# Three orders in a fused RWKV and feed-forward kernel: shifts behind scales, weight loads earlier, one late step rearranged

## The chip, the cores and the metric

The kernel runs on one core of a Trainium2 chip. The metric is the device time of one execution in microseconds (us). The engines are TensorE (PE in the profile, PEld for its weight loads), VectorE (DVE), ScalarE (ACT), GpSimd (POOL) and SyncE (SP), which here only issues DMAs.

## What is computed

The first half is RWKV-6 attention over 4 batches, 8 heads, 768 tokens and a head dimension of 48; the second half a feed-forward block with 384 model and 2048 hidden columns, whose activation is h times erf of softplus of h.

```python
for t in range(S):
    kt, vt, rt, wt = (k[:, :, t], v[:, :, t], r[:, :, t], w[:, :, t])
    cur = np.einsum('bhd,bhe->bhde', u[None] * kt, vt)
    y[:, :, t] = np.einsum('bhd,bhde->bhe', rt, state + cur)
    state = wt[:, :, :, None] * state + np.einsum('bhd,bhe->bhde', kt, vt)
...
h = x @ w_in
sp = np.maximum(h, 0.0) + np.log1p(np.exp(-np.abs(h)))
g = h * erf(sp)
return (g @ w_out).astype(np.float32)
```

The weights `w_in` and `w_out` come as 64-bit floats, and the kernel makes them 32-bit floats on the chip.

## The kernel before, in words

**Steps.** The tokens are worked off in 12 steps, s = 0 to 11. A step holds 128 tokens of two batches (16 heads), and one tile `in` with r and k, one `w` and one `v`. The first step has a function of its own, `attend_first` (L833); steps 1 to 4 go through `attend` (L962), steps 5 to 11 through `attend_late` (L782). The second step of the change is s = 1, the sixth s = 5. Beside the attention of step s, TensorE works on the feed-forward block of earlier steps in pieces: a piece of `hidden` (L1087) of step s - 1 is 12 matmuls with `w_in_sb` (line L1120 in the profile) and one ScalarE copy out of PSUM (L1129); its PSUM tiles are two that take turns. A piece of `project_fast` (L1227) of step s - 3 is 8 matmuls with `w_out_sb` or `mixed` (L1242).

**Levels of a step.** In `attend` the tokens within a block of 64 are handled in levels 1 to 6. A level is 64 small matmuls (`level_products`, L641) on r and k, then `scale` (L334, VectorE), which multiplies r and k in place by products of w so that the next level's matmuls can use them, then `take_level`, which copies the products where a mask holds: on VectorE up to level 5 (L651), at level 6 by two ScalarE copies (L658). After level 6, `from_own` (L673) multiplies the result with v. `prepare` of the next step is a generator whose parts are run in between: among them GpSimd's totals of w (L408) and ScalarE's products with u (L386, L389).

**Conversion of the weights.** `convert` (L223) cuts w_in and w_out into 8 chunks each, chunks 0 to 7 being w_in. A chunk goes through these stages, which the code names by letters:
- `l`, load (L231): two DMAs of 384 KB into a tile `words`, of which there are three, taking turns. A load can be made to wait by a marker, a copy of one element into the tile on GpSimd (L244) or ScalarE (L242).
- `b`, the base (L259 for w_in): ScalarE, from `words` into PSUM. From chunk 2 on all bases use the one tile `y`.
- `r`, the low words (L267): ScalarE, from `words` into `rest`, of which there are two.
- `h`, the shift (L276): VectorE, from the base into the weights.
- `o`, the add (L289): GpSimd, adds `rest`.

Piece n of the hidden work of step 0 needs chunk n whole. In the second step, chunks 2 to 7 are converted while the levels run. At each level from 2 on, a GpSimd copy of one element of k (L994) makes the adds wait until `scale` is done.

**Order of the work.** All engines' orders are written out by hand: each engine takes its instructions in the order of the program, DMAs on SP's queue too. An instruction that waits holds up what stands behind it on its engine. In the second step, `place(n)` is called after each level; it sends bases, low words and loads by the table `CONVERT` (L1477), then one hidden piece.

**The late steps.** In `attend_late`, the function `run` (L1566) works off a string of tokens at seven places ("front", "near", 0 to 4), from `USUAL` or, for a step that has an entry there, from `LATE`. `P` is a project piece, `H` a hidden piece, `F` the next part of `prepare` of the next step (in the sixth step, among others, the scales of levels 1 to 3 of the seventh), `s` a softplus on a chunk of hidden values (L1076, with a table load), `ey` and `ep` the erf of it into the tile `y` or a bank `pp` (L1080), `m` the VectorE multiply that follows (L1085). `kABx` copies a quarter of the hidden values of step s - 2 to lane x, `y` or `pp`, in PSUM (L1200), and `S1` to `S4` are VectorE sums of quarters (L1219 to L1225). Pieces 3, 4, 6 and 7 of a project end with a copy or an add out of PSUM: L1253 (piece 3) and L1256 (piece 4) on ScalarE, L1262 (piece 6) and L1267 (piece 7) on VectorE. The PSUM tiles of the project are those that the hidden pieces take next.

Of the kernel before, what the change touches and what calls it, by code (L numbers as in the profile page):

```python
# [17 lines left out]
P = 128  # L18
# [22 lines left out]
DIRECT = 4  # L41
# [21 lines left out]
def kernel(  # L63
# [23 lines left out]
    KT = DM // P  # L87
# [65 lines left out]
    def load_w(s):  # L153
        ws[s] = ins.tile([P, JP, C], FP32, name="w")
        nc.sync.dma_start(out=ws[s][:], in_=rkw[s][:, 2])
# [34 lines left out]
    def load_v(s):  # L190

        vt = loaded[s][1]
        nc.sync.dma_start(out=vt[:], in_=v[s])
# [493 lines left out]
    def through_state(s, xT):  # L687

        c, in_t, _, _, S, _, _ = parts_of(s)
        for h, state in enumerate((S, middle)):  # L690
            if not (c or h):
                continue
            t = slice(h * HC, (h + 1) * HC)
            for j, q in ((0, 2), (1, 2), (1, 0), (0, 0)) if not s else np.ndindex(NJ, NP // 2):
                q = q if not s else 2 * q
                for e in range(NE):
                    for p in (q + e, q + 1 - e):
                        n = j * NP + p
                        nc.tensor.matmul(  # L699
                            y[at(e, p), e, p // 2, j, t],  # L700
                            lhsT=state[rows(e), n, :],
                            rhs=(in_t[:, 0, n] if s else first_pair(0, n))[rows(e), t],
                            start=False, stop=True, skip_group_check=True,
                        )

        y3 = att.tile([P, UNIT], FP32, name="y3", bufs=1)
        nc.scalar.copy(y3[:].rearrange("p (j t) -> p j t", j=NJ), y[:, 1, 1])
        parts = y[:, 0, 0], y[:, 0, 1], y[:, 1, 0]
        by_kk = [xT[:, kk, :].rearrange("p (j t) -> p j t", j=NJ) for kk in range(KT)]
        if not s:  # L710

            def hop():
                for kk in range(KT):
                    nc.tensor.matmul(
                        parts[kk], lhsT=apart[:, kk],
                        rhs=y3[:].rearrange("p (j t) -> p j t", j=NJ),
                        start=False, stop=True, skip_group_check=True,
                    )
                for kk in range(KT):
                    nc.scalar.copy(by_kk[kk], parts[kk])  # L720
                stages["l"](3, xT[:, KT - 1, 0:1], True)
                stages["l"](4)
                load_w(2)

            turns["hop"] = hop
            return
        for kk in range(KT):
            nc.scalar.copy(by_kk[kk], parts[kk])
        by_scalar = {(kk, 1) for kk in range(KT) if s <= DIRECT}
        for kk in range(KT):  # L730
            n = D // KT
            for e in range(NE):
                queue = nc.scalar if (kk, e) in by_scalar else nc.sync
                queue.dma_start(
                    out=xT[e * EP + D : (e + 1) * EP, kk, :],
                    in_=y3[e * EP + kk * n : e * EP + (kk + 1) * n, :],
                )
# [95 lines left out]
    def attend_first(xT):  # L833
# [5 lines left out]
        c, _, vt, made, S, S_next, ends = parts_of(0)  # L839
# [73 lines left out]
        stages["b"](1, 1)  # L913
        fence()
        stages["l"](2, seen[:, 0:1])
        load_v(1)
        stages["h"](0)
        stages["h"](0)
        ps = [[products([P, NE, JP, HC], 1 - e)[:, e] for e in range(NE)]]
# [15 lines left out]
        def pending():  # L935
            part = products([P, NE, JP, HC], turns["next"])[:, 0]
            state_part(0, kT, ps + [[part] * NE], (1,))
            nc.vector.tensor_add(S_next[both], faded[1][both], part[both, :, :D])
            load_third()
            stages["l"](5, S_next[:, 0, 0:1])  # L940

        turns["pending"] = pending

# [18 lines left out]
    def attend(s, xT, early, place, behind):  # L962

        c, in_t, vt, made, S, S_next, ends = parts_of(s)
        K = in_t[:, 1]
        RK = by_pair(in_t)


        following = prepare(s + 1) if s + 1 < n_steps else iter(())
        own = made if s >= DIRECT else att.tile([P, NH, HC], FP32, name="own")  # L970

        if s == DIRECT:
            next(following)
        for level in range(near_log(s) + 1 if s == DIRECT else 1, LOG + 1):
            rk = by_pair(made) if level == 1 else RK
            pp = turns.pop("pp", None) or products([P, NE, JP, HC])
            if s == level == 1:
                level_products(pp, rk, level, range(NP))
                turns.pop("hop")()
                level_products(pp, rk, level, range(NP, JP))  # L980
                send("br")
            elif s != 2 or level != 2:
                level_products(pp, rk, level)
            if level == LOG and s == DIRECT:
                spread_blocks(s + 1, pp)
            if s == 1 and 2 < level:
                stages["h"](level + 1)
            scale(s, level)
            if s == 1 and level == 2:
                turns.pop("pending")()  # L990
            if s == 1 and level < 3:
                stages["h"](level + 1)
            if s == 1 and level > 1:
                nc.gpsimd.tensor_copy(out=block_sb[:, 0:1], in_=K[:, 0, 0:1])  # L994
                for i in {2: (2, 3)}.get(level, (level + 1,)):
                    stages["o"](i)
            if s != 1:
                early(level - 1)
            got = pp[:].rearrange("p e n t -> p (e n) t")
            if level == 1:  # L1000
                nc.vector.tensor_mul(
                    own[:], got, first[:, None, :].to_broadcast([P, NH, HC])
                )
            else:
                take_level(own, pp, level)
            later_on = (s, level) in ((1, 4), (DIRECT, LOG))
            if level > 1 and not later_on:
                next(following, None)
            if (s, level) == (DIRECT, LOG - 1):
                next(following, None)  # L1010
            if s == 2 and level == 1:

                def ahead():
                    turns["pp"] = products([P, NE, JP, HC])
                    level_products(turns["pp"], RK, 2)

                turns["ahead"] = ahead
            place(level - 1)
            if later_on:
                next(following, None)  # L1020
            if (s, level) == (DIRECT - 1, LOG - 1):
                nc.gpsimd.tensor_copy(out=first[:, 0:1], in_=own[:, 0, HC // 4 : HC // 4 + 1])
                mixing.send(nc.gpsimd)
            if s == 1 and level in (3, 4):
                nc.sync.dma_start(out=loaded[2][0][:, level - 3], in_=rkw[2][:, level - 3])

        from_own(s, own, 1)
        ps = products([P, JP, P])
        for n in range(JP):
            nc.tensor.transpose(ps[:, n, :], K[:, n, :], ident[:])  # L1030
        kT = att.tile([P, NH, D], FP32, name="kT", bufs=1)
        nc.scalar.copy(
            kT[:].rearrange("p (e n) d -> p e n d", e=NE),
            ps[:].rearrange("p n (e d) -> p e n d", e=NE)[..., :D],
        )
        if c:
            nc.gpsimd.tensor_mul(
                faded[0][:], S[:], ends[:, :, 0:1].to_broadcast([P, JP, D])
            )
        next(following, None)  # L1040
        place(LOG)
        if s == 2:
            mixing.send(nc.vector)
        if s == DIRECT - 1:
            advance(1)

        ps = products([P, NC, JP, HC])
        ps = [[ps[:, h]] * NE for h in range(NC)]
        state_part(s, kT, ps)
        from_own(s, own, 0)  # L1050
        if c:
            nc.vector.tensor_add(middle[both], faded[0][both], ps[0][0][both, :, :D])
        else:
            nc.vector.tensor_copy(middle[both], ps[0][0][both, :, :D])
        if s == DIRECT - 1:
            blend(s - 2, 1)
        nc.gpsimd.tensor_mul(faded[1][:], middle[:], ends[:, :, 1:2].to_broadcast([P, JP, D]))
        nc.vector.tensor_add(S_next[both], faded[1][both], ps[1][0][both, :, :D])
        for _ in following:
            pass  # L1060
        place(LOG + 1)
        through_state(s, xT)
        behind()
# [356 lines left out]
    def in_order(s, k):  # L1420
# [7 lines left out]

    STAGES_LATE = ("front", "near", 0, 1, 2, 3, 4)
    LATE = {  # L1430
        n_steps - 1: (
            "s P", "m w", "ey P m s P P ep P", "m P P", "", "", ""
        ),
# [71 lines left out]
    with tc.manual_schedule(  # L1505
# [78 lines left out]
        s = n_steps  # L1584
# [108 lines left out]
```

## Time and profile before

| what | us |
|---|---|
| median of 3 runs | 577.24 |
| lowest and highest of them | 577.05 and 582.2 |
| the profiled execution's own time | 579.45 |
| its span, from the first to the last instruction | 577.7 |
| PE busy | 568.4 |
| DVE busy | 441.9 |
| ACT busy | 357.8 |
| POOL busy | 245.9 |

Times in the profile count from the start of the span. A line of the timeline gives the start, the duration, the engine, the line of the kernel, the operation, its output and inputs with their sizes, how many instructions are merged, and in brackets how long the engine was idle before it and whose end released it. A line of the waits gives who waited, for whom, the sum in us, how often, and the longest. The granted TensorE clock was 0.999 of full speed over the span.

### The profile page before, as it was taken

The page shows a single profiled execution, that of the slowest core. Times are in us where ns is not written, and L with a number is a line of the kernel's source. Part 1 is how long each engine was busy: PE and PEld are TensorE (multiplying, and loading weights), DVE is VectorE, ACT ScalarE, POOL GpSimd, SP SyncE. Part 2 cuts the span into 40 slices and gives each one's busy share as a digit, 9 for nine tenths or more (in the row PEclk, how much of TensorE's full clock was granted, in tenths as well). Part 3 has the DMA queues.
Part 4 walks back from the last instruction along what each step waited for, and adds up shares of the span by engine and source line. Part 5 has one row for each costly group of instructions (what it writes and reads, how often), then busy time and mean ns, then how long its engine had stood idle before and what let it go on. Part 6 is the DMA issues. An engine that isn't in the chain of part 4 may idle for free.

```text
span 577.7 us, 16717 instructions
## 1 busy us (share of the span) xinstructions
PE 568.4 (98%) x7336; PEld 503.7 (87%) x7336; DVE 441.9 (76%) x475; ACT 357.8 (62%) x488; POOL 245.9 (43%) x265
## 2 busy tenths in 40 slices
PE   8999999999999999999999999999999999999997
PEld 6677787678998988998998998898898899988997
DVE  8766786999899998699699599599599527256640
ACT  3648877645458847757756766766766661388700
POOL 4557381632885884384284185175173000000000
PEclk9999999999999999999999999999999999999999
DMA  8696671440436315145245235234232201000000
GB/s 265 188 332 228 206 232 45 188 159 8 146 70 180 108 58 164 35 156 169 34 143 175 40 126 191 39 112 167 43 111 82 48 8 37 1 1 2 27 28 27
DMA packets 54081, 63.24 MB, mean 109 GB/s; under 512 B 35160, under 2 KB 40568, under 8 KB 52984
## 3 DMA queue, kind: packets, MB, share of 16 engines
q1 hardware_dynamic: 53624, 61.98, 34.4%
q8 instruction: 57, 0.93, 0.7%
q10 hardware_dynamic: 384, 0.20, 0.1%
q14 instruction: 16, 0.13, 0.1%
HBM read 52.39 MB, written 8.69 MB: 106 GB/s over the span
## 4 chain that ended last, share of the span: by engine, by line
PE 85%; DVE 3%; issue 0%; DMA 0%; POOL 0%; ACTq 0%; DVEq 0%; POOLq 0%
PE m L1120 33%; PE m L1242 32%; PE pp L1330 4%; PE m L1152 4%; PE pp L641 4%; PE y L1330 2%; PE y L673 2%; PE y L699 2%; PE pp L748 1%; DVE h L1085 1%; PE pp L1030 1%; PE pp L1242 0%; DVE sums L529 0%; DVE in L334 0%; DVE words L494 0%
## 5 line engine op out<-in xcount | busy, mean ns | idle before, releaser
L1120 PE MATMUL m<-xT,w_in_sb 128*128 128x256 f32 x960 | 215.4, 382 | 0.3 <-DMA xT<-y 0.2
L1120 PEld LDWEIGHTS m<-xT,w_in_sb 128*128 128x128 f32 x960 | 179.7, 190 | 26.4 <-ACT h L1129 1.0
L334 DVE TENSOR_TENSOR in<-in,tot_sb 128x1024 f32<-128x1024 f32 (+1 forms) x55 | 78.8, 1432 | 12.5 <-PE pp L641 11.1
L1129 ACT COPY h<-m 128x512 f32<-128x512 f32 x80 | 46.3, 578 | 48.2 <-PE m L1120 47.9
L1242 PE MATMUL m<-mixed,h 128*128 128x192 f32 x320 | 56.7, 331 | 0.0
L1242 PE MATMUL m<-w_out_sb,h 128*128 128x192 f32 x320 | 56.1, 329 | 0.0
L1242 PE MATMUL m<-w_out_sb,room 128*128 128x192 f32 x304 | 52.6, 326 | 0.7 <-ACT o L1253 0.7
L1242 PEld LDWEIGHTS m<-mixed,h 128*128 128x128 f32 x320 | 51.8, 190 | 1.0
L1242 PEld LDWEIGHTS m<-w_out_sb,h 128*128 128x128 f32 x320 | 52.0, 190 | 0.5
L1242 PEld LDWEIGHTS m<-w_out_sb,room 128*128 128x128 f32 x304 | 49.9, 190 | 1.0 <-ACT o L1253 1.0
L1080 ACT ACT_TABLE_LOAD x30 | 38.5, 1283 | 9.1 <-DVE h L1085 8.6
L641 PEld LDWEIGHTS pp<-in 48*48 48x48 f32 (+4 forms) x2368 | 30.1, 120 | 12.5 <-issue 6.1
L463 POOL TENSOR_TENSOR words<-words,own 128x384 f32<-128x384 f32 x21 | 31.0, 1475 | 22.7 <-DVE words L494 13.0
L504 POOL TENSOR_TENSOR words<-words 128x384 f32<-128x384 f32 x28 | 39.7, 1447 | 0.0
L1076 ACT ACT_TABLE_LOAD x30 | 38.5, 1283 | 1.8 <-issue 1.3
L456 POOL TENSOR_TENSOR own<-rest 128x384 f32<-128x384 f32 x7 | 9.7, 1384 | 61.5 <-ACT o L1248 61.5
L641 PE MATMUL pp<-in 48*48 48x32 f32 (+4 forms) x2368 | 33.9, 206 | 1.9 <-DVE in L334 1.9
L504 POOL TENSOR_TENSOR rk<-words 128x384 f32<-128x384 f32 x28 | 33.4, 1221 | 0.0
L529 DVE TENSOR_REDUCE sums<-rk 128x16 f32<-128x768 f32 (+2 forms) x31 | 31.6, 1021 | 0.0
L408 POOL TENSOR_TENSOR tot_sb<-tot_sb 128x256 f32<-128x256 f32 (+4 forms) x50 | 28.8, 576 | 3.8
L1076 ACT ACTIVATE room<-h 128x1024 f32<-128x1024 f32 x28 | 29.6, 1057 | 0.3
L1200 ACT COPY y<-h 128x1024 f32<-128x1024 f32 x12 | 12.2, 1018 | 26.7 <-DVE h L1085 16.9
(206 smaller groups left out, 997.2 us busy)
## 6 DMA issues: line engine op xcount, KB each, us to landing
in<-in_rkw SPq DMA_DIRECT2D x8, 1024.0 KB, 5.3
words<-in_moe_w_in SPq DMA_DIRECT2D x16, 384.0 KB, 6.8
words<-in_moe_w_out SPq DMA_DIRECT2D x16, 384.0 KB, 5.4
words<-in_rk_rows SPq DMA_DIRECT2D x8, 768.0 KB, 6.9
w<-in_rkw SPq DMA_DIRECT2D x11, 512.0 KB
v<-in_v SPq DMA_DIRECT2D x12, 384.0 KB, 5.7
out<-o SPq DMA_DIRECT2D x23, 192.0 KB, 3.2
in<-in_rkw SPq DMA_DIRECT2D x7, 512.0 KB, 5.3
```

The source lines that it names most:

```text
L334: nc.vector.tensor_mul(halves, halves, view(tots[level - 1], 0, [[1, n], [2, nb], [0, half]]))
L408: nc.gpsimd.tensor_mul(new, pair[:, :, 0], pair[:, :, 1])
L463: engine.tensor_mul(to, to, of[:, :, None, :].to_broadcast([P, NEAR // 2 // half, half, D]))
L504: engine.tensor_mul(to[:, i], r[:, half:], k[:, part * rows + i, None].to_broadcast([P, half, D]),)
L529: nc.vector.tensor_reduce(out=to, in_=of, axis=mybir.AxisListType.X, op=ALU.add)
L641: nc.tensor.matmul(to, lhsT=rk(1, n)[rows(e), s0 : s0 + m], rhs=right, start=True, stop=True,)
L1076: nc.scalar.activation(sp_room, chunks[0], AF.Softplus)
L1080: nc.scalar.activation(at, sp_room, AF.Erf)
L1120: nc.tensor.matmul(ps[:, ff, :], lhsT=w_in_sb[:, g * FG + f + ff, kk * P : (kk + 1) * P], rhs=xT[:, kk, :], start=kk == 0, stop=kk == KT - 1,)
L1129: nc.scalar.copy(h[:, f : f + FT, :], ps[:])
L1242: nc.tensor.matmul(to, lhsT=a[:, f], rhs=b[:, f], start=start and f == 0, stop=f == FG - 1, skip_group_check=True,)
L1330: nc.tensor.matmul(to[:, e], lhsT=a[:, 2 * i + e], rhs=b, start=start and not k, stop=True, skip_group_check=True,)
```

## The change

In `hop`, at level 1 of the second step, the loads of chunks 3 and 4 and of w of the third step become the load of chunk 4 alone, with the ScalarE marker that chunk 3 had. Chunk 3 is loaded in the first step, behind chunk 2, without a marker, where v of the second step stood. Chunk 5, which waited for the new state by a GpSimd marker, is loaded at the end of level 1 without a marker. w of the third step and v of the second are loaded at the end of level 3.

At levels 3 to 6 of the second step the shift goes from ahead of `scale` to behind `take_level`, and the marker copy of k and the add go behind the shift. Level 2 keeps its order.

The sixth step gets an entry in `LATE`. Against `USUAL`, a `P` goes ahead of the `s` at place 0, and two `F` go from the end of place 1 to behind `S1` at place 2.

```diff
@@ hop
-                stages["l"](3, xT[:, KT - 1, 0:1], True)
-                stages["l"](4)
-                load_w(2)
+                stages["l"](4, xT[:, KT - 1, 0:1], True)
@@ attend_first
         stages["l"](2, seen[:, 0:1])
-        load_v(1)
+        stages["l"](3)
@@ pending
             load_third()
-            stages["l"](5, S_next[:, 0, 0:1])
@@ attend
                 send("br")
+                stages["l"](5)
             elif s != 2 or level != 2:
                 level_products(pp, rk, level)
             if level == LOG and s == DIRECT:
                 spread_blocks(s + 1, pp)
-            if s == 1 and 2 < level:
-                stages["h"](level + 1)
             scale(s, level)
             if s == 1 and level == 2:
                 turns.pop("pending")()
             if s == 1 and level < 3:
                 stages["h"](level + 1)
-            if s == 1 and level > 1:
+            def add_up():
                 nc.gpsimd.tensor_copy(out=block_sb[:, 0:1], in_=K[:, 0, 0:1])
                 for i in {2: (2, 3)}.get(level, (level + 1,)):
                     stages["o"](i)
+
+            if s == 1 and level == 2:
+                add_up()
...
                 take_level(own, pp, level)
+            if s == 1 and level > 2:
+                stages["h"](level + 1)
+                add_up()
...
             if s == 1 and level in (3, 4):
                 nc.sync.dma_start(out=loaded[2][0][:, level - 3], in_=rkw[2][:, level - 3])
+                if level == 3:
+                    load_w(2)
+                    load_v(1)
@@ LATE
     LATE = {
+        DIRECT + 1: (
+            "s P", "m", "ey P m P s P ep P", "m k22y P F P k11p", "S1 F F",
+            "S2 S3 H k12y S4 H F", "s H ey m H H F s H ep H H",
+        ),
...
     USUAL = (
         "s P", "m", "ey P m s P P ep P", "m k22y P F P k11p F F", "S1", "S2 S3 H k12y S4 H F",
         "s H ey m H H F s H ep H H",
     )
```

## The prediction

> **What bounds the kernel now.** I read the page's busy shares and its chain first: TensorE (PE) sets the time. Then the waits of PE, asked for in stretches of the span, to find where it is not full; then the timeline of the two stretches that the change touches.
>
> ```profile
> PE 568.4 (98%) x7336; PEld 503.7 (87%) x7336; DVE 441.9 (76%) x475; ACT 357.8 (62%) x488; POOL 245.9 (43%) x265
> PE 85%; DVE 3%; issue 0%; DMA 0%; POOL 0%; ACTq 0%; DVEq 0%; POOLq 0%
> ```
>
> The 2% that PE is idle is all there is to win by order alone. Its waits by stretch (engine and line waiting, who released it, us in total, times, longest): the second step lies in 28 to 64 us, the sixth in 191 to 236.
>
> ```profile
> PE pp L641 <- DVE in L334: 1.9, 2, 1.2
> ...
> PE m L1242 <- ACT o L1253: 0.7, 1, 0.7
> PE m L1120 <- DVE o L1262: 0.2, 1, 0.2
> ...
> PEld m L1120 <- ACT h L1129: 1.0, 3, 0.4
> ```
>
> Between 64 and 191 us PE waits 0.2 us in all, between 236 and 533 not at all. So what PE gains in the two steps should last to the end. The second step, in order of time (start, duration, engine, line):
>
> ```profile
> 37.83 0.96 DVE L276 TENSOR_SCALAR w_in_sb<-y 128x768 int32<-128x768 int32 x1 [1.26 <-ACT y L259]
> 38.70 1.22 DVE L334 TENSOR_TENSOR in<-in,tot_sb 128x1024 f32<-128x1024 f32 x1
> 39.97 1.03 PE L641 MATMUL pp<-in 48*56 48x32 f32 x64 [1.18 <-DVE in L334]
> ...
> 44.52 0.92 PE L641 MATMUL pp<-in 48*48 48x32 f32 x64 [0.73 <-DVE in L334]
> 44.67 1.82 POOL L289 TENSOR_TENSOR w_in_sb<-w_in_sb,rest 128x768 int32<-128x768 int32 x1
> ...
> 45.86 1.71 DVE L334 TENSOR_TENSOR in<-in,tot_sb 128x1024 f32<-128x1024 f32 x1
> ...
> 47.38 0.90 ACT L259 ACTIVATE y<-words 128x768 f32<-128x768 f32 x1
> ...
> 49.25 1.80 POOL L289 TENSOR_TENSOR w_in_sb<-w_in_sb,rest 128x768 int32<-128x768 int32 x1
> 49.32 2.81 DVE L334 TENSOR_TENSOR in<-in,tot_sb 128x1024 f32<-128x1024 f32 x1
> 49.48 1.17 ACT L658 COPY own<-pp 32x512 f32<-32x512 f32 x2
> ```
>
> See two things. The shift (L276) waits for ScalarE, ScalarE for a weight load, and the scale (L334) that PE needs stands behind it. And a scale beside a GpSimd add (L289) ends 1.08 us after that add: 47.57 after 46.49, 52.13 after 51.05. Alone it takes 1.22. So one excludes the other. The sixth step:
>
> ```profile
> 203.23 2.87 PE L1242 MATMUL m<-w_out_sb,room 128*128 128x192 f32 x16 [0.75 <-ACT o L1253]
> ...
> 213.46 21.62 PE L1120 MATMUL m<-xT,w_in_sb 128*128 128x256 f32 x96 [0.16 <-DVE o L1262]
> ...
> 212.86 0.54 DVE L1262 TENSOR_TENSOR o<-o,m 128x384 f32<-128x384 f32 x1
> ...
> 215.10 3.50 DVE L334 TENSOR_TENSOR in<-in,tot_sb 128x1024 f32<-128x1024 f32 x2
> 218.52 1.21 DVE L1219 TENSOR_TENSOR room<-h,y 128x1024 f32<-128x1024 f32 x1
> ...
> 219.76 1.02 ACT L1200 COPY y<-h 128x1024 f32<-128x1024 f32 x1 [2.82 <-DVE room L1219]
> 220.71 0.58 ACT L1129 COPY h<-m 128x512 f32<-128x512 f32 x1
> ```
>
> Two scales hold up S1 (L1219), S1 the lane copy (L1200), this the second hidden copy (L1129). The 96 matmuls take 21.62 us; in the chain the next step's 96 take 20.92.
>
> **Second step, what PE could gain.** Each level is 64 products, then 12 matmuls of hidden work. With 2.79 us for these, level 4's products could start at 35.93 + 2.79 = 38.72 instead of 39.97, level 5's 0.80 sooner after its own hidden work: 2.05 us.
>
> **What the new order allows.** At levels 3 to 6 it is scale, mask copy (L651), shift, add. I follow it.
> - Level 2: scale ends 33.21 as before. The GpSimd marker L244 for load 5 is gone, so the two adds (3.60 us together) run from 33.41 to 37.01, not to 37.65.
> - Level 3: scale can start at 36.0 (products end 35.97), but lies beside the second add, so it ends about 38.1; in time for PE at 38.72. Then the mask copy starts 1.01 after the add's end (as 47.50 after 46.49), shift 4 0.62 later (45.00 after 44.38) and takes 0.96: it ends at 37.01 + 1.01 + 0.62 + 0.96 = 39.60.
> - Level 4: scale could start at 39.82 (products end 39.75, and VectorE follows PE by 0.07). Add 4 starts 0.14 after its shift (as 65.62 after 65.48): 39.74. These lie 0.08 us apart, and my working is no finer than 0.1. Whoever is first delays the other.
> - GpSimd first: add to 41.56, scale to 42.64; level 5 starts at 42.69, 0.22 late. Shift 5 ends 44.15, ScalarE takes base 6 (0.88), its low words (0.91), a hidden copy (0.57) and the next step's u products, which took 1.75 from 45.63 to 47.38. Base 7 then starts at 48.0, not 47.38. From base 7 to the start of the level-6 copies (L658) is 2.10 in the trace, and these take 1.17: they end at 51.3, and PE's from_own, at 51.63 before, starts about 51.35. Gain **0.25**.
> - VectorE first: scale 4 is done at 41.0, add 4 runs to 42.8, add 5 to 44.77 and scale 5 (due at 43.46) ends at 45.8. Shift 6 ends 47.36, base 7 starts at 47.4, as before, the copies end at 50.7, from_own starts at 50.75. Gain **0.88**.
>
> So ScalarE's copies at level 6, hidden today (done 50.65, needed 51.63), become the limit: every shift now comes behind a scale, and each base waits for the shift before it, as they share the tile y. Neither exclusion happening would be the upper end: shift 6 at 46.2, base 7 at 46.6, from_own at 49.9, gain 1.7.
>
> On this exclusion the Trainium skill ("SBUF — State Buffer", section "Who interferes with whom") says that a VectorE instruction with two SBUF inputs contends with a GpSimd instruction that reads SBUF, and that issue order decides who blocks. The two ends above agree with it; by it the sum is 0.25 or 0.88, without it 1.7.
>
> **Loads moved on SP's queue.** Load 3 (two of 384 KB) takes the place of v of the second step at 23.2; its tile's last reader ended at 12.8. Load 4 keeps ScalarE's marker at 28.2. Load 5 waits for ScalarE's reads of its buffer (29.8), not for the state at 33.8. Load 6 follows at 31.8, then half of the third step's input, w and v, with SP free and none needed before 44.8 (w: the totals, L408; v: from_own). A load takes 3.2 to 7.8 us to land here; load 4 is needed at 34.6 (load 3, issued at the same moment before, was used at 33.44), load 5 at 39.6, load 6 at 42.6, load 7 at 47.4, all inside. Cost nothing; if load 7 came later than base 7, PE pays from 48.36 on (51.63 less 2.10 and 1.17). Nothing behind them on SP is wanted earlier than before.
>
> **Adds.** Add 5 ends 44.8 to 47.1 and PE wants it at 46.8 to 47.2, add 6 50.2 to 51.8 against 52.3 to 52.9: at most 0.1, inside time that PE waits anyway.
>
> **Sixth step.** (1) The softplus goes behind one more product, so the copy L1253 goes ahead of it and PE's 0.75 at 203.23 goes. But the first hidden piece needs L1262, which stands in a VectorE row without gaps from 191.95 to 213.40, in the same order as before. PE waits 0.91 there instead of 0.16: **0**. (2) S1 moves ahead of the two scales: S1 215.10 to 216.31, lane copy 216.93 (behind the first hidden copy), second hidden copy when PE is done, about 218.9 instead of 220.71. The next softplus, third copy, erf and fourth copy follow at about 219.4, 221.8, 223.6 and 224.6; TensorE wants the two buffers at 223.9 and 226.5. The three weight-load waits go: 21.62 - 20.92 = **0.70**. The scales pass to 216.2, beside a GpSimd fade that ran 215.65 to 217.51; the last ends at about 219.2, `middle` (L824, 219.65) is not later. At worst, if the fade costs a scale 1.3 more, the erf is 0.5 later and the fourth copy still ends before 226.5. Lower bound 0, if another wait takes the slot.
>
> **Sum.** 0.25 + 0 + 0.70 = 0.95. The profiled execution took 579.45 (span 577.7 and 1.75 around it): 578.5 for a like one. It lies 2.21 above the median, 577.24; from the median the forecast is 576.3.
>
> **Rivals.**
> - VectorE first at level 4: 0.88 + 0.70 = 1.58, 575.7. For it: the two starts lie within my error, and at 193.81 an equal start went to VectorE. Against: the add comes out 0.08 earlier.
> - The exclusion hardly bites, 1.7 + 0.70 = 2.4: 574.8. Against: three scales beside adds (24.34 is another, ending 26.02 after 24.93).
> - No gain: in one of the two steps another wait takes all, 577.0 (0.25 alone).
> - Slower: base 7 is late. Both exclusions going GpSimd's way put shift 6's end at 48.7, from_own at 52.05, 0.42 later than before; it is slower in sum only once base 7 starts after 49.06 (48.36 + 0.70), by load 7 landing over 12 us after its issue at 36.4. For it: 896 KB of w and v now stand ahead of it. Against: 7.8 us is the longest. At 50.0: 578.2.
>
> **How the numbers follow.** Forecast 0.45, VectorE first 0.28, no exclusion 0.08, no gain in one step 0.12, slower 0.07. The range 574.6 to 577.2 holds all cases but the slower one, with the 0.2 between the two lower runs shown (577.05, 577.24) added at each end. A measurement of this kernel tells about 1% (5.8 us) from no change. All waits of PE in both steps, 1.9 + 0.9 + 1.0, sum to less, so faster by over 1% is 0.01; slower by over 1% needs a wait that I do not see, 0.03; within 1% 0.96.
>
> **What would show it.** Right: PE's two waits for L334 in the second step shrink to 0.3 or less, and a new one of 0.5 to 2 us stands ahead of from_own (L673), released by L658. Scales at levels 3 and 4 or 5 take over 1.7 us beside an add. In the sixth step the wait for L1253 is gone, that for L1262 is about 0.9, and the 96 matmuls take 20.9. Wrong: no wait at L673, a ScalarE base (L259) that waits for a load, or the 96 still at 21.6.

## The result, and the profile after

| | before | after |
|---|---|---|
| median of 22 runs each, us | 578.09 | 580.66 |
| lowest, us | 576.74 | 579.30 |
| profiled execution, its own time, us | 579.45 | 580.04 |
| its last 240 project matmuls begin, us | 533.00 | 533.58 |

The kernel became slower: the ratio after to before is 1.004, 95% interval 1.0029 to 1.0052. The forecast was 0.95 us less; the medians show 2.6 us more. The two profiled executions differ by 0.6 us only, because that of before was a late one. A second profile of before, below, begins its last 240 matmuls at 531.38, 2.2 us ahead of after.

Busy time hardly changed. In the chain that ended last GpSimd and VectorE now hold 17%, but that is no sign of the loss: in the fastest kernel below ("loads and sixth step") they hold 16%. From the page after:

```profile
PE 567.6 (98%) x7336; PEld 504.0 (87%) x7336; DVE 442.8 (77%) x475; ACT 357.9 (62%) x488; POOL 246.3 (43%) x264
PE 75%; POOL 9%; DVE 8%; issue 4%; ACT 3%; POOLq 0%; DVEq 0%
```

TensorE's waits after, in the stretches of the second, the third to fifth and the sixth step (who waits, for whom, us in total, times, longest). Lines behind the changed ones are 5 higher in this kernel, so L1125 and L1134 are the hidden pieces' L1120 and L1129; the marker copy of k, L994 before, is L990:

```profile
PE y L673 <- ACT h L1134: 2.7, 1, 2.7
PE pp L641 <- DVE in L334: 0.2, 1, 0.2
...
PE m L1125 <- ACT h L1134: 0.3, 1, 0.3
PE pp L641 <- DVE in L334: 0.2, 1, 0.2
...
PE m L1125 <- DVE o L1267: 1.0, 1, 1.0
```

The waits that the change aimed at are gone (1.9 for the scale in the second step is 0.2, 0.75 for L1253 in the sixth is nothing). A new one of 2.7 us stands ahead of from_own, two small ones of 0.3 and 0.2 between 64 and 191 us, and the sixth step has 1.0 where 0.16 was. The timeline after shows what from_own waits for:

```profile
39.57 1.83 POOL L289 TENSOR_TENSOR w_in_sb<-w_in_sb,rest 128x768 int32<-128x768 int32 x1 [1.36 <-DVE w_in_sb L276]
39.74 2.75 DVE L334 TENSOR_TENSOR in<-in,tot_sb 128x1024 f32<-128x1024 f32 x1 [0.31 <-PE pp L641]
44.09 2.68 POOL L289 TENSOR_TENSOR w_in_sb<-w_in_sb,rest 128x768 int32<-128x768 int32 x1 [1.36 <-DVE w_in_sb L276]
46.74 1.03 POOL L408 TENSOR_TENSOR tot_sb<-w 128x512 f32<-128x512 f32 x1
47.84 0.91 ACT L259 ACTIVATE y<-words 128x768 f32<-128x768 f32 x1
47.85 0.61 POOL L408 TENSOR_TENSOR tot_sb<-tot_sb 128x256 f32<-128x256 f32 x1
48.41 0.18 POOL L990 COPY block_sb<-in 128x1 f32<-128x1 f32 x1
48.55 1.81 POOL L289 TENSOR_TENSOR w_in_sb<-w_in_sb,rest 128x768 int32<-128x768 int32 x1
48.63 2.81 DVE L334 TENSOR_TENSOR in<-in,tot_sb 128x1024 f32<-128x1024 f32 x1 [2.07 <-POOL block_sb L990]
49.92 1.17 ACT L658 COPY own<-pp 32x512 f32<-32x512 f32 x2
51.37 0.94 DVE L276 TENSOR_SCALAR w_in_sb<-y 128x768 int32<-128x768 int32 x1
52.41 0.66 PE L673 MATMUL y<-own,v 64*48 64x64 f32 x32 [2.69 <-ACT h L1134]
```

Read it from the end. The wait is put down to a hidden copy (L1134), but that one starts at 51.11 and takes 0.59. What ends 0.10 us ahead of from_own is the shift, 51.37 + 0.94 = 52.31: it reads the tile y, which from_own overwrites. The shift stands behind scale 6. Scale 6 waited 2.07 us for the GpSimd copy L990, which reads the element of k that the scale overwrites. That copy had its turn only at 48.41, behind the add of 44.09 and two totals of w (L408). Then it lay beside the add of 48.55. ScalarE's level-6 copies, the limit of my forecast, ended at 51.09.

To set kernels side by side, their profiles are cut at the same instructions (us):

| kernel | level 3 to from_own, second step | level 3 of the third step to the next step's first project piece | level-5 products to from_own, sixth step |
|---|---|---|---|
| before, profiled with the prediction | 16.73 | 24.94 | 44.01 |
| before, again | 15.67 | 24.94 | 43.97 |
| after | 17.64 | 25.72 | 43.20 |
| after, again | 17.66 | 25.73 | 43.19 |

Against the second profile of before, after loses 1.97 and 0.78, wins 0.77, and loses 0.22 in stretches between: 2.20 = 533.58 - 531.38.

### The profile page after: what moved, and what is told of

Its sections match the earlier page's. It is cut to its first block, busy times and chain, and to the rows that moved or that the text cites. A ratio compares the mean times of both kernels' runs of the same rounds, so it can differ in the third digit from the quotient of the medians.

```text
span 578.2 us, 16715 instructions
## 1 busy us (share of the span) xinstructions
PE 567.6 (98%) x7336; PEld 504.0 (87%) x7336; DVE 442.8 (77%) x475; ACT 357.9 (62%) x488; POOL 246.3 (43%) x264
## 4 chain that ended last, share of the span: by engine, by line
PE 75%; POOL 9%; DVE 8%; issue 4%; ACT 3%; POOLq 0%; DVEq 0%
PE m L1247 29%; PE m L1125 27%; PE pp L1335 4%; PE pp L641 4%; POOL tot_sb L408 3%; PE y L1335 2%; DVE in L334 2%; PE m L1157 2%; PE y L673 2%; PE y L699 1%; POOL words L504 1%; PE pp L746 1%; PE m L945 1%; POOL rk L504 1%; DVE words L494 1%
## 5 line engine op out<-in xcount | busy, mean ns | idle before, releaser
L1125 PE MATMUL m<-xT,w_in_sb 128*128 128x256 f32 x960 | 214.6, 382 | 1.4 <-DVE o L1267 1.0
L1125 PEld LDWEIGHTS m<-xT,w_in_sb 128*128 128x128 f32 x960 | 180.0, 190 | 26.4 <-DVE o L1267 1.1
L334 DVE TENSOR_TENSOR in<-in,tot_sb 128x1024 f32<-128x1024 f32 (+1 forms) x55 | 81.4, 1480 | 14.2 <-PE pp L641 10.7
L1134 ACT COPY h<-m 128x512 f32<-128x512 f32 x80 | 46.2, 580 | 48.6 <-PE m L1125 48.4
L408 POOL TENSOR_TENSOR tot_sb<-tot_sb 128x256 f32<-128x256 f32 (+4 forms) x50 | 29.1, 582 | 3.8
L1247 PE MATMUL m<-mixed,room 128*128 128x192 f32 x160 | 27.7, 327 | 0.0
```

What stands on the lines that cost most here:

```text
L334: nc.vector.tensor_mul(halves, halves, view(tots[level - 1], 0, [[1, n], [2, nb], [0, half]]))
L408: nc.gpsimd.tensor_mul(new, pair[:, :, 0], pair[:, :, 1])
L1125: nc.tensor.matmul(ps[:, ff, :], lhsT=w_in_sb[:, g * FG + f + ff, kk * P : (kk + 1) * P], rhs=xT[:, kk, :], start=kk == 0, stop=kk == KT - 1,)
L1134: nc.scalar.copy(h[:, f : f + FT, :], ps[:])
L1247: nc.tensor.matmul(to, lhsT=a[:, f], rhs=b[:, f], start=start and f == 0, stop=f == FG - 1, skip_group_check=True,)
```

## The experiments

Ratios are to the kernel before, run on the same chip, with a 95% interval.

**Before, again** (no edit).

> The kernel before, unchanged, for a second profile and for the clock of each run. All theories: ratio 1.000. The kernel after was 2.3 us longer than before by the medians, but its profiled execution only 0.6 us longer than that of before. If the profiled execution of before was a late one, this one ends its last matmul near 573 us instead of 574.6, and the place of the difference shows where before can lose time by chance: the third step (64 to 93 us), where a scale and a GpSimd add start 0.1 us apart, is the first guess.

0.9984 (0.997 to 0.9998), median 578.04. An unchanged kernel thus lands 0.16% off, with 1 just outside its interval: differences under about 1 us I judge by the cuts in the profile. The place was not the third step, as guessed, but the second. Its two waits for the scale, 1.9 us in the first profile, are here

```profile
PE pp L641 <- DVE in L334: 0.9, 1, 0.9
```

and in the profiles of six further kernels with the old second step ("sixth step only", "next parts only", "softplus only", and before with one idle matmul of each of three sizes) no such line is there: 14.7 to 15.0 us from level 3 to from_own. Nearly all that was to be won in the second step was the bad luck of one execution. In the first profile the shift waits for ScalarE and ScalarE for a load; ScalarE's waits for loads sum to 7.3 us there, to 5.7 here and to 4.6 to 6.1 in the six others. That the landing of the loads sets TensorE's waits is likely by this but not shown, since the 6.1 went without one.

**Shifts only, loads only, sixth step only**: each the kernel before with one part of the diff shown above.

> Of the change only the order at levels 3 to 6 of the second step: scale, mask copy, shift, marker, add. Loads and sixth step as before. Theory A (shift 7 behind scale 6 keeps TensorE from the tile y): from_own (L673) waits over 2 us as in the kernel after and starts at 52.2 or later; 1 to 3 us slower than before. Theory B (the moved loads do the harm): no wait over 0.5 us at from_own, and 0.2 to 0.9 us faster than before.

> Of the change only the loads: chunk 3 earlier, chunk 5 without a marker, w and v later; shifts ahead of the scales as before. Theory A: the shift no longer waits for a load at levels 3 and 4, so TensorE's two waits for the scale (1.18 and 0.73 us) shrink to under 0.4 together, and the time is 1 to 2 us under before. Theory B: ScalarE's bases wait for loads, slower than before by 1 us or more.

> Of the change only the entry for the sixth step. Theory A: the 96 hidden matmuls of that step take 20.9 to 21.0 us instead of 21.6, TensorE waits 0.9 to 1.0 us ahead of them for the VectorE add instead of 0.16, none for the ScalarE copy; 0.6 to 0.8 us faster than before. Theory B (the entry costs time, for the kernel after is slower by more than its second step explains): same or slower than before.

| part alone | ratio | second step | third | sixth |
|---|---|---|---|---|
| shifts | 1.002 (1.000 to 1.004) | 16.67 | 25.73 | 43.83 |
| loads | 0.9994 (0.9976 to 1.0012) | 14.66 | 24.94 | 43.83 |
| sixth step | 0.998 (0.9964 to 0.9996) | 15.02 | 24.94 | 43.30 |

The loss is the shifts'. With them alone TensorE waits 1.85 us at from_own, a little under the forecast of over 2. In this profile VectorE was first at level 4 (scale at 40.99, add at 41.21), the better of the two cases in the prediction, and from_own (52.44) still came behind shift 7 (done at 52.33). The loads do what was wanted: ScalarE's waits for loads between 28 and 64 us, of before and of loads only:

```profile
ACT y L259 <- DMA words<-in_moe_w_in: 7.3, 3, 3.6
```

```profile
ACT y L259 <- DMA words<-in_moe_w_in: 0.2, 1, 0.2
```

and no wait of TensorE's is listed in that stretch. The forecast of 1 to 2 us less missed all the same (0.9994), as six of the eight profiles of the old second step have no such wait either. With the shifts ahead of the scales, base 7 starts 10.2 us behind level 3 with these loads; in the kernel after, with the same loads, 13.1.

The profile of shifts only shows a further cost. Three stretches of it (from:to, length, busy us and instructions of PE, PEld, DVE, ACT, POOL, then the granted clock, DMA share and GB/s):

```profile
49.80:52.40 2.60, 0.78 (x4) 0.35 (x2) 2.54 (x2) 2.42 (x5) 2.44 (x4) 1.00 0.68 262
53.30:56.70 3.40, 3.40 (x14) 2.93 (x13) 0.00 (x0) 1.92 (x6) 1.31 (x1) 0.51 0.02 5
56.70:60.00 3.30, 3.30 (x106) 2.73 (x105) 0.56 (x1) 3.27 (x4) 0.00 (x0) 0.99 0.00 0
```

Behind the wait the granted clock is 0.51 for 3.4 us, and the 12 hidden matmuls there take 3.85 us instead of 2.76. One such stretch makes the mean clock of an execution 0.997. No profile of the kernel after holds one: both its profiled executions have the wait of 2.7 us and the full clock behind it. But of its 22 executions 12 have a mean of 0.996 or 0.997 (median 581.00) and 10 have 0.999 or 1.0 (median 579.61), while of the 116 executions of the kernel before beside all the experiments 4 have 0.997.

**Shift 7 ahead** (in after):

```diff
             elif s != 2 or level != 2:
                 level_products(pp, rk, level)
...
+            if s == 1 and level == LOG:
+                stages["h"](level + 1)
             scale(s, level)
...
             if s == 1 and level > 2:
-                stages["h"](level + 1)
+                if level < LOG:
+                    stages["h"](level + 1)
                 add_up()
```

> The kernel after, but at level 6 of the second step the shift stands ahead of the scale again, as before. Theory A (in the kernel after from_own waits for shift 7, the last reader of the tile y, behind scale 6): TensorE's wait of 2.7 us at L673 shrinks to about 1.4, now for the ScalarE copies of level 6 alone (they ended at 51.1); from level 3 to from_own 16.3 to 16.5 us instead of 17.6; 1 to 2.5 us faster than the kernel after, near the kernel before. Rival (ScalarE's copies are what it waits for, as forecast): wait and time as in the kernel after.

**No marker at level 5** (in after):

```diff
             def add_up():
-                nc.gpsimd.tensor_copy(out=block_sb[:, 0:1], in_=K[:, 0, 0:1])
+                if level != 5:
+                    nc.gpsimd.tensor_copy(out=block_sb[:, 0:1], in_=K[:, 0, 0:1])
```

> The kernel after without the one GpSimd marker copy at level 5 of the second step, which reads k and so holds scale 6 back until GpSimd comes to it. Theory A: scale 6 starts about 46.9 instead of 48.6, takes under 1.5 us, shift 7 ends by 49.8, and from_own waits 1.4 us for ScalarE instead of 2.7; 1 to 2.5 us faster than the kernel after. Rival (scale 6 waits for its products or for the port, not for the marker): scale 6 at 48.5 and the time as in the kernel after.

Medians 578.49 and 578.68, 2.0 to 2.2 below after; ratios 1.0007 (0.9995 to 1.0019) and 1.002 (0.9999 to 1.004). From level 3 to from_own 15.78 and 15.80 us, third step 24.95 and 24.94. Lines of the second:

```profile
46.71 1.88 DVE L334 TENSOR_TENSOR in<-in,tot_sb 128x1024 f32<-128x1024 f32 x1 [0.41 <-PE pp L641]
48.54 0.96 DVE L276 TENSOR_SCALAR w_in_sb<-y 128x768 int32<-128x768 int32 x1
49.68 1.17 ACT L658 COPY own<-pp 32x512 f32<-32x512 f32 x2
50.30 0.32 PE L673 MATMUL y<-own,v 64*48 64x64 f32 x4 [0.85 <-ACT own L658]
50.90 0.65 PE L673 MATMUL y<-own,v 64*48 64x64 f32 x28 [0.28 <-ACT own L658]
```

Without the marker scale 6 starts 1.65 us sooner, counted from level 3 (12.21 against 13.86). It takes 1.88, not under 1.5 as expected, but shift 7 is done at 49.5, and what is left is the limit I had forecast: from_own follows the ScalarE copies, its first four matmuls already the first of them. That is better than my 1.4 us of wait (1.1 in both), and it is no better than before (15.67, or 14.7 to 15.0 without bad luck). So the rivals fall, and the order has nothing to give even with its worst fault mended.

The profiled execution of shift 7 ahead is the slowest of its 13 (582.25, mean clock 0.997). Its half clock is not behind from_own. It stands in the first step, behind a pause of 1.64 us in which TensorE waited for nothing that the profile shows; over 5 us the granted clock is 0.66:

```profile
20.92 0.77 PE L641 MATMUL pp<-in 48*32 48x32 f32 x63 [1.64 <-issue]
20.00:25.00 5.00, 4.08 (x79) 2.97 (x82) 1.36 (x3) 1.63 (x3) 0.00 (x0) 0.66 0.08 29
```

**Loads and sixth step** (shifts left ahead of the scales).

> The moved loads and the entry for the sixth step, shifts ahead of the scales as before. All theories that put the loss on the shifts: second step without waits (14.7 us from level 3 to from_own), sixth with 20.9 to 21.0 us for its hidden matmuls; last project matmuls from about 530.2 us; 1.0 to 1.7 us faster than before. If loads and entry harm together: not faster than the entry alone, 0.998 of before.

0.9982 (0.9967 to 0.9996), median 576.90, the fastest kernel here: second step 14.66, third 24.95, sixth 43.20; last 240 matmuls from 530.46, 0.92 ahead of before, again. By the medians it lies 1.2 us under before, little more than the 0.8 that the copy of before showed by chance. Level 3 to from_own wins 1.01 against that copy and the sixth step 0.77; 0.88 is lost ahead of level 3 of the second step, which starts at 35.51 instead of 34.63.

**After, again** (no edit).

> The kernel after, unchanged, for a second profile. Theory A: again a wait of 2 us or more at from_own of the second step (L673), and 17 to 18 us from level 3 to from_own; a third or more of the executions with a mean clock of 0.997; 1.003 to 1.005 of before. In the third step the scale and the GpSimd add at level 3 start within 0.1 us again, and either can be first. Rival: the wait was a chance of that one execution, under 1 us here.

1.0058 (1.004 to 1.0076), median 580.64. The wait at L673 is 2.69 us again, 17.66 us from level 3, and 3 of 6 executions have 0.996 or 0.997. It was no chance.

**Idle matmuls in the wait** (in after): five, and then three.

```diff
-        from_own(s, own, 1)
         ps = products([P, JP, P])
+        if s == 1:
+            for _ in range(5):
+                nc.tensor.matmul(
+                    ps[:].rearrange("p n t -> p (n t)")[:, :DM], lhsT=ident[:],
+                    rhs=states[1][0][:].rearrange("p n d -> p (n d)"),
+                    start=True, stop=True, skip_group_check=True,
+                )
+        from_own(s, own, 1)
```

> The kernel after with five idle matmuls (128x384, about 0.46 us each) on TensorE ahead of from_own in the second step, where it waits; their result is overwritten. Theory A (about half of the executions of the kernel after show a mean clock of 0.997, because TensorE's wait of 2.7 us lets the granted clock fall to a half for 3.4 us): no execution under 0.999, median 0.6 to 1.3 us under the kernel after, and nothing else changed. Rival (the lower clock comes from elsewhere): as many executions at 0.997 as before, time the same or up to 0.3 us longer.

> The kernel after with three idle matmuls ahead of from_own in the second step instead of five: five took 3.3 us and ended 0.7 us behind the wait that they were to fill. Theory A: from_own starts when shift 7 is done, as in the kernel after (17.6 us behind level 3), no execution below a mean clock of 0.999, median 0.5 to 1.2 us below the kernel after. Rival (the low clock is not from this wait): executions at 0.997 as often as in the kernel after, about half.

With five, all 6 executions have 0.999 or 1.0, but the median is 580.83: the five take 3.3 us and end 0.7 us behind shift 7, and this kernel's TensorE also starts level 3 1.1 us later, behind a pause of 1.0 us in which it waited for nothing that the profile shows. So the first forecast of the time missed. With three, from_own comes 17.66 us behind level 3 as in after, its wait is 0.76, 11 of 12 executions have 0.999 or more, and the median is 579.57, about that of after's executions at full clock (579.61). So the low clock of after's executions comes from the wait. Its price is best read from after's own executions: 580.66 for all against 579.61 at full clock, about 1 us in the median. The ratio with three, 1.0033 (1.0018 to 1.0049), overlaps with after's and does not show the gain by itself. Not every low clock comes from this wait: kernels without it have up to 3 such executions in 10 (with 128x96, below).

**Third step, TensorE late**: the kernel before with one idle matmul ahead of level 3 of the third step, 128x384, 128x96 and 128x192.

```diff
+                if s == 2 and level == 3:
+                    nc.tensor.matmul(
+                        pp[:].rearrange("p e n t -> p (e n t)")[:, :DM], lhsT=ident[:],
+                        rhs=states[1][0][:].rearrange("p n d -> p (n d)"),
+                        start=True, stop=True, skip_group_check=True,
+                    )
                 level_products(pp, rk, level)
```

> The kernel before with one idle matmul (128x384, about 0.45 us) on TensorE ahead of the level-3 products of the third step; its result is overwritten. In the kernel before the scale there starts 0.08 us ahead of a GpSimd add; in the kernel after, with TensorE later, 0.04 us behind it. Theory A (who is first decides, and the late scale costs about 0.8 us up to the first project piece): the scale comes behind the add and takes over 2 us, and from level 3 to the first project piece it takes 0.45 + 0.8 us more than the 24.94 of before. Rival (the 0.8 us come from something else that late TensorE work does not bring about): 0.45 us more, or less.

> As the run with one idle matmul ahead of level 3 of the third step, but 128x96 instead of 128x384, so that TensorE is some 0.1 to 0.2 us late. Theory A (a scale that starts just behind the GpSimd add pays nearly the whole add; 0.65 us behind it, as with the larger matmul, it pays little): the scale takes 2.6 us or more, and from level 3 to the first project piece it takes 0.5 to 0.8 us more than 24.94. Rival: 0.2 us more or less.

> The same with an idle matmul of 128x192. 128x96 made TensorE 0.09 us late and scale and add started together, with the scale first; 128x384 made it 0.46 late and cost 0.18 from level 3 to the first project piece. Theory A: here TensorE is about 0.2 late, the scale starts about 0.1 behind the add and pays nearly all of it: 2.7 us or more, and 0.5 to 0.8 us more than 24.94 to the first project piece, more than with twice the delay. Rival (the loss grows with the delay): 0.1 us or less.

The scale of level 3 and the GpSimd add, in before again, in after, and with 128x192:

```profile
68.19 1.23 DVE L334 TENSOR_TENSOR in<-in,tot_sb 128x1024 f32<-128x1024 f32 x1
68.30 2.81 POOL L289 TENSOR_TENSOR w_out_sb<-w_out_sb,rest 128x768 int32<-128x768 int32 x1 [1.56 <-DVE w_out_sb L281]
```

```profile
70.15 2.86 DVE L334 TENSOR_TENSOR in<-in,tot_sb 128x1024 f32<-128x1024 f32 x1 [0.19 <-PE pp L641]
70.11 1.82 POOL L289 TENSOR_TENSOR w_out_sb<-w_out_sb,rest 128x768 int32<-128x768 int32 x1 [1.57 <-DVE w_out_sb L281]
```

```profile
67.98 2.79 DVE L334 TENSOR_TENSOR in<-in,tot_sb 128x1024 f32<-128x1024 f32 x1 [0.26 <-PE pp L641]
67.86 1.82 POOL L289 TENSOR_TENSOR w_out_sb<-w_out_sb,rest 128x768 int32<-128x768 int32 x1 [1.57 <-DVE w_out_sb L281]
```

| idle matmul | TensorE later by | scale behind add by | scale takes | loss up to the first project piece |
|---|---|---|---|---|
| 128x96 | 0.09 | 0.00, scale first | 1.23 | 0.00 |
| 128x192 | 0.23 | 0.12 | 2.79 | 0.71 |
| 128x384 | 0.46 | 0.65 | 2.26 | 0.18 |

(A delay is the stretch from the third step's level 2 to its level 3 against the 6.70 of before, again; losses are against 24.94.) Each row is one profile. Both first forecasts missed: the loss of 1.25 us expected at 128x384 was 0.18, as a scale that comes well behind the add pays only its rest, and at 128x96 the scale was still first. The last run is the test, and a larger delay costs less than a smaller one, as the turn explains. Ratios 1.0014 (0.9999 to 1.0029) and 1.0017 (0.9999 to 1.0035) for 128x384 and 128x96; 128x192 ran once, 578.32 beside 578.01.

In the kernel after, though, it is not a later TensorE that turns the order. Counted from level 2 of the third step, its level 3 comes at 6.55 (6.70 in before, again), its scale at 7.70 (7.85) and the add at 7.66 (7.96): the add comes 0.30 sooner, the scale, which waits for TensorE's products, only 0.15. The 0.30 stems from ScalarE, which issues two DMAs of xT in 1.18 us instead of 1.47 and so starts the base (L261) 0.42 us behind level 2 instead of 0.73. After, and before again:

```profile
61.64 1.18 ACTq L732 DMA_DIRECT2D xT<-y  x2
62.87 0.86 ACT L261 ACTIVATE y<-words 128x768 f32<-128x768 f32 x1 [1.40 <-issue]
```

```profile
59.55 1.47 ACTq L734 DMA_DIRECT2D xT<-y  x2
61.07 0.86 ACT L261 ACTIVATE y<-words 128x768 f32<-128x768 f32 x1 [1.70 <-issue]
```

All four profiles in which from_own waits for shift 7 (after twice, shifts only, three idle matmuls) have these issues in 1.18 to 1.32 us and the loss of 0.78 or 0.79. The others have 1.35 to 1.70 and no such loss, but for 128x384 with 1.19 (its add, too, came 0.30 sooner) and 128x192. With five idle matmuls from_own comes later still, 18.23 us behind level 3, and the third step takes 24.94. So the turn is shown to cost the 0.78, and why the issues are shorter in these kernels is open.

**The sixth step's two edits apart** (before, with one of them in the entry).

> The kernel before with only the two next parts (F F) behind S1 in the sixth step. Theory A: this is all of the sixth step's gain: 20.9 to 21.0 us for the 96 hidden matmuls, the wait of 0.75 us for the ScalarE copy of piece 3 stays, that for the VectorE add stays near 0.2 to 0.3; 0.6 to 0.7 us faster than before in this step. Rival (both edits are needed): 21.4 us or more.

> The kernel before with only the softplus of the sixth step one product later. Theory A: the 0.75 us wait goes and comes back ahead of the hidden matmuls (1.0 us for the VectorE add there), which take 21.6 us as before; no change in time (within 0.1 us in this step). Rival: 0.5 us or more faster in this step.

Next parts only: sixth step 43.18 us, ratio 0.9999 (0.9985 to 1.0012); softplus only: 43.82, 1.0002 (0.9985 to 1.0018); before, again: 43.97. Their hidden matmuls:

```profile
211.00 20.99 PE L1120 MATMUL m<-xT,w_in_sb 128*128 128x256 f32 x96
```

```profile
212.25 21.62 PE L1120 MATMUL m<-xT,w_in_sb 128*128 128x256 f32 x96 [0.99 <-DVE o L1262]
```

All of the step's gain comes from the two `F` behind `S1`. Of the time as a whole 0.8 us is too little for these ratios to show.

## Why the prediction was wrong, step by step

- **"What the new order allows", case GpSimd first: failed at its end.** Up to level 5 it was followed closely: adds to 36.9 (forecast 37.0), add 4 ahead of scale 4, scale 4 to 42.49 (42.6), base 7 at 47.84 (48.0), the level-6 copies 49.92 to 51.09 (to 51.3). But I put the end of these copies as what from_own waits for. I had written that the bases share the tile y, and did not follow that from_own overwrites it: its last reader, shift 7, had moved behind scale 6. And I read the 2.81 us of the scale at 49.32 of before as a scale beside an add, without asking why it started at 49.32: the marker copy of the level before reads what it overwrites, and had no term in my sum. Before, that late scale held up nothing of TensorE's; now shift 7 stands behind it. Term forecast as a gain of 0.25; measured a loss of 1.97 against before, again, and 0.91 even against the late profile that I started from.
- **"What PE could gain", 2.05 us: its base failed.** The waits were those of one execution. In seven further profiles of the old second step they are 0.9 once and nothing six times. I had noted that this execution lay 2.21 above the median, and took the gain off the median all the same.
- **"So what PE gains ... should last": failed for losses.** In the third step a GpSimd add came 0.30 us sooner, and the scale went from 0.1 us ahead of it to 0.04 behind: 0.78 us. In the waits this stretch looked full, 0.2 us idle in 127. What made the add come sooner is followed only as far as ScalarE's DMA issues.
- **The clock** was not in the prediction: about half of the executions with the wait of 2.7 us have a mean clock of 0.996 or 0.997, which costs about 1 us in the median. The Trainium skill ("TensorE: Matmul & The Clock Gate", section "HAM oscillation — how this bites in real kernels") gives as a rule no idle gaps over about 3.4 us; in the traces here half the clock followed gaps of 1.85 us (shifts only) and 1.64 us (shift 7 ahead), and the measurement decides.
- **Loads, "cost nothing": right.** Load 7 was in time, ScalarE's bases wait for no load after.
- **Sixth step: right.** The softplus edit is worth nothing (wait moved to the VectorE add, 1.00 against 0.91 forecast), the two scales 0.70 forecast and 0.77 measured. After:

```profile
214.66 20.99 PE L1125 MATMUL m<-xT,w_in_sb 128*128 128x256 f32 x96 [1.00 <-DVE o L1267]
...
216.31 1.21 DVE L1224 TENSOR_TENSOR room<-h,y 128x1024 f32<-128x1024 f32 x1
217.44 2.77 DVE L334 TENSOR_TENSOR in<-in,tot_sb 128x1024 f32<-128x1024 f32 x2
...
218.04 1.02 ACT L1205 COPY y<-h 128x1024 f32<-128x1024 f32 x1
220.15 0.59 ACT L1134 COPY h<-m 128x512 f32<-128x512 f32 x1 [1.09 <-PE m L1125]
```

  S1 now comes ahead of the two scales, the lane copy right behind the first hidden copy, and the second hidden copy waits for TensorE instead of holding it up.
- **The slower rival** had the right place (from_own, GpSimd's turns) and the wrong cause: no load was late, and base 7 started at 47.84, where shift 7 started only at 51.37. Its from_own at 52.05 lay below the 52.41 measured.
- **"A measurement of this kernel tells about 1%": too coarse.** The interval of the result is 1.0029 to 1.0052, and the loss of 0.4% stands clear of no change.

## What to carry to other kernels

Before an instruction is moved behind another, list who overwrites what it reads, and what that other instruction itself waits for, writes after reads included: the stall sits with the last reader of a shared tile, not with the work that looks long. Count a wait as something to win only if a second execution shows it too, above all where a load may set it. Where two engines exclude each other and start within 0.1 us, 0.2 to 0.3 us upstream on either side can flip the turn, so a full stretch is not a safe one.

## What was not expected of the hardware

- A granted clock of one half for over 3 us followed a TensorE gap of 1.85 us in the profile of shifts only and one of 1.64 us in that of shift 7 ahead, but none of the gaps of 2.7 us in the two profiles of after. 15 of the 28 executions of after have a mean clock such as one such stretch gives, and 1 of 12 with the wait filled to 0.76. What picks the executions was not tried.
- When a scale and a GpSimd add started at the same recorded time (67.19, with the idle matmul of 128x96), VectorE went first (1.23 us) and the add took 2.91; 0.04 us behind the add, in after, the scale took 2.86 and the add 1.82.
- Four profiles have a pause of TensorE in which it waits for nothing that the profile shows: about 1.0 us at level 1 of the second step (shifts only, five idle matmuls), and 1.15 and 1.64 us at level 6 of the first step (softplus only, shift 7 ahead). Its cause stays open.
